# Thirty seven-product groups instead of twenty-five in a speech joint network, with a longer ring and evictions placed by the scheduler

## The chip, the cores and the metric

The kernel runs on one core of a Trainium2 chip. A core has five engines that run beside each other, each through its own queue in order: TensorE (PE, matrix products into PSUM), VectorE (DVE), ScalarE (ACT), GpSimd (POOL) and SyncE (SP, which here only issues transfers). The metric is the device time of one execution in microseconds, as a median of several runs.

## The reference, cut to what matters

Two audio sequences x of 4000 steps and 512 channels go through two convolutions of five taps, each followed by a gelu and by taking every second step; 1000 steps f per sequence are left. Eight label vectors g per sequence come beside them. Both are projected, every step is combined with every label by a tanh, and the result is projected again:

```
f  = gelu(conv5(gelu(conv5(x, w1))[::2], w2))[::2]      # (2, 1000, 512)
fe = f @ w_f;  ge = g @ w_g                              # (2, 1000, 512), (2, 8, 512)
j  = tanh(fe[:, :, None, :] + ge[:, None, :, :])         # (2, 1000, 8, 512)
out = j @ w_o                                            # (2, 1000, 8, 512)
```

All operands are bf16. The last line is 16000 rows of 512 by a matrix of 512 x 512.

## The kernel before, in words

**Stages.** The first convolution and most of the second fill about the first half of the time. They use transforms that need fewer products than five taps; one unit of the second convolution (class `Unit`, steps `s1` to `s5`) makes nine times four products of 334 columns for one batch and one quarter of the channels, evicted by ACT and DVE. `fe` (L908) projects f: eight times four products of 501 columns per batch, evicted by ACT for odd and by DVE for even quarters m.

**The joint stage.** The 16000 rows (label by label, 1000 steps each) are cut into 125 tiles of 128. `tanh(v, k)` (L919) makes, on ACT, the k-th quarter of the channels of label v: 1000 columns, 64 such calls. It writes into a ring jT of 3072 columns, so a call that crosses the ring's end is cut in two; a slot can be written again only when the products that read it are done.

**Plain tiles.** `Plain.go` (L1034) makes one tile with four products of 512 columns, one eviction to ost and the store.

**Groups of seven products.** `Seven` makes four tiles together, as a 2 x 2 block product in Strassen's manner (Winograd's form): seven products of half size instead of eight. Each is four matmuls of 256 columns (two row tiles, two k). Its operands are tiles of jT, sums of tiles (`sums`, L1062: three on POOL that follow from each other, one on DVE, all into one of four buffers ss, in fp16) and sums of quarters of w_o (tw, made once on POOL). Of the seven results, three are copied from PSUM to SBUF (`keep`, buffers sn), three are added to such a copy by DVE into the output buffer og (`out` with v), one is copied to og (`p4`). A bank is used further after its copy: product 6 adds to the bank of product 1 once that was copied, 7 to that of 6, 4 to that of 7 once DVE has added it, 3 to that of 5.

**Order.** The loop at L1186 gives the groups in this order: p1 of a group, p7 of the one before, p5, p2, a filler, the sums of the next group, p6, p4 of the one before, p3, a filler. Fillers are, for the first 13 groups, what is left of the second convolution and fe of the second batch (18 pieces), and then two plain tiles for each of ten groups. The last two groups have none. After the fe of the first batch (L1168) come the rest of conv unit 12 and 13, then two plain tiles, then the groups.

**The scheduler.** This order is not yet that of the engines. `Plan.schedule` (L150) is a list scheduler with a cost for each instruction: for PE, POOL and SP it takes, of the instructions that are ready, the first in the order written; for ACT and DVE the one with the earliest due time. Before, each instruction's engine is fixed when it is written: products 1, 6 and mostly 5 are copied by ACT, plain tiles by DVE, product 4 mostly by DVE.

The functions that the diff touches, with the profile's line numbers:

Of the kernel before, what the change touches and what calls it, by code (L numbers as in the profile page):

```python
# [63 lines left out]
class Op:  # L64
    __slots__ = ("eng", "fn", "reads", "writes", "dma", "signal", "count", "sem", "val", "idx", "cost", "pin", "after", "wire")


class Plan:
# [11 lines left out]
    def op(self, eng, fn, reads=(), writes=(), cost=0.1):  # L80
        o = Op()
        o.eng, o.fn, o.dma, o.signal, o.idx = eng, fn, False, False, len(self.ops)
        o.reads, o.writes, o.cost, o.pin, o.after = tuple(reads), tuple(writes), cost, self.pin, list(self.hold)
        self.ops.append(o)
        return o

    def dma(self, eng, fn, reads=(), writes=(), sem=None, nbytes=524288, rate=345e3):

        o = Op()
        o.eng, o.fn, o.dma, o.signal, o.idx = eng, fn, True, False, len(self.ops)  # L90
        o.reads, o.writes, o.cost, o.pin, o.after, o.wire = tuple(reads), tuple(writes), 0.43, True, [], nbytes / rate
        if sem is None:
            sem = [self.nc.alloc_semaphore(f"s_d{o.idx}"), 0]
        sem[1] += 16
        o.sem, o.val = sem[0], sem[1]
        self.ops.append(o)
        return o

    def edges(self):
# [26 lines left out]
        for o in ops:  # L126
            p = {}
            for j in np.flatnonzero(sbuf[o.idx, :o.idx] | psum[o.idx, :o.idx]).tolist():
                q = ops[j]
                if o.dma and q.dma and not set(x for v in o.writes for x in v.cells.tolist()) & set(  # L130
                        x for v in q.reads + q.writes for x in v.cells.tolist()):
                    continue
                same = q.eng == o.eng and not q.dma and not o.dma
                over = any(W[o.idx, c] > R[o.idx, c] and R[j, c] + W[j, c] > 0 or R[o.idx, c] > 0 and W[j, c] > 0
                           for c in range(na, na + 8))
                p[j] = not same or (bool(sbuf[o.idx, j] or over) and o.eng != "pe")
            for j in o.after:
                if ops[j].eng != o.eng or ops[j].dma:
                    p[j] = True
                else:  # L140
                    p.setdefault(j, False)
            if o.pin:
                j = last.get(o.eng)
                if j is not None:
                    p.setdefault(j, False)
                last[o.eng] = o.idx
            pred.append(p)
        return pred

    def schedule(self, pred):  # L150
# [20 lines left out]
        cand = {e: [] for e in free}  # L171
        for i in range(n):
            if not left[i]:
                cand[ops[i].eng].append(i)
        order = {e: [] for e in free}
        wire, start = 0.0, [0.0] * n
        for _ in range(n):
            best = None
            for e, c in cand.items():
                if c:  # L180
                    t = max(free[e], min(ready[i] for i in c))
                    if best is None or t < best[0]:
                        best = (t, e)
            t, e = best
            now = [i for i in cand[e] if ready[i] <= t + 0.02]
            i = min(now, key=(lambda i: i) if e in ("pe", "sp", "pool") else (lambda i: (late[i], i)))
            cand[e].remove(i)
            order[e].append(i)
            o = ops[i]
            start[i] = t  # L190
            free[e] = t + o.cost
            end = free[e]
            if o.dma:
                wire = max(wire, t + 1.8) + o.wire
                end = max(wire, t + 2.0)
            for s in succ[i]:
                ready[s] = max(ready[s], end + HOP if pred[s][i] else free[e])
                left[s] -= 1
                if not left[s]:
                    cand[ops[s].eng].append(s)  # L200
# [4 lines left out]
    def emit(self, block, tail):  # L205
        nc, ops = self.nc, self.ops
        pred = self.edges()
        order = self.schedule(pred)
        pos = {i: p for e in order for p, i in enumerate(order[e])}
# [69 lines left out]
def bass_standalone__seq2seq_rnn_t_joint__speech_kernel(  # L279
# [29 lines left out]
    RING = 3072  # L309
# [5 lines left out]
    with ExitStack() as es:  # L315
# [45 lines left out]
        jT = at("jT", [NK, RING], BF16, w1_off)  # L361
# [556 lines left out]

        def tanh(v, k):  # L919

            b, u = v // U, v % U
            lo, hi = v * T2, (v + 1) * T2
            while lo < hi:
                n = min(hi - lo, RING - lo % RING)
                t = lo - v * T2
                act(jT[k, lo % RING:lo % RING + n], feT[b][k, t:t + n], ACT.Tanh,
                    bias=geT[k * BU + v:k * BU + v + 1])
                lo += n
# [50 lines left out]
        nu = len(units) - 2  # L979
# [28 lines left out]
        def evict(eng, o, v):  # L1008
            if eng == "act":
# [15 lines left out]
        class Plain:  # L1025
# [8 lines left out]
            def go(self, last=False):  # L1034
                r0, s = self.jt * P % RING, self.s
                for h in range(2 if last else 1):
                    w = H if last else NT
                    cl = slice(h * w, (h + 1) * w)
                    bk = take()
                    v = ps.cols(bk * NT, w)  # L1040
                    mm(v, [(jT[k, r0:r0 + P], wo_sb[k, cl]) for k in range(NK)], True, True)
                    evict("act" if h else "dve", ost[s][cl], v)
                    free.append(bk)
                    store(self.jt, lambda a, b: ost[s].rows(a, b, cl), ("p", s), ("sp", "act")[h], cl)

        class Seven:
# [4 lines left out]
            def __init__(self, jt):  # L1051
                self.jt, self.n = jt, Seven.count
                Seven.count += 1
                assert jt % 2 == 0 and RING % (2 * P) == 0
                self.c = [(jt + 2 * r) * P % RING for r in range(2)]
# [3 lines left out]
            def a(self, r, k):  # L1059
                return jT[2 * k:2 * k + 2, self.c[r]:self.c[r] + H]  # L1060

            def sums(self):  # L1062
                S = self.S
                for eng, i, x, y, op in (("pool", 0, self.a(1, 0), self.a(1, 1), add),
# [3 lines left out]
                    tt(eng, S[i], x, y, op)  # L1068

            def product(self, i, bk, start, check=False):  # L1070

                tile = lambda r, t, k: jT[k, self.c[r] + t * P:self.c[r] + (t + 1) * P]
# [35 lines left out]
            def p1(self):  # L1108
                self.A = take()
                self.product(1, self.A, True)  # L1110
                self.s1 = self.keep("act", self.A)

            def p5(self):
                self.D = take()
                self.product(5, self.D, True)
                self.d5 = self.keep("dve" if self.n < NF and self.n % 2 == 0 else "act", self.D)
# [7 lines left out]
            def p6(self):  # L1124
                self.product(6, self.A, False)
                self.u2 = self.keep("act", self.A)
# [11 lines left out]
            def p4(self, last=False):  # L1138
                self.product(4, self.A, False)
                self.out(1, 0, self.A, None, "act" if self.n >= NF and self.n % 4 == 0 else "dve")  # L1140
# [3 lines left out]
        pend, state = [], [1, 0]  # L1144

        def tanhs(upto, spread=None):

            while state[0] < B * U and not pend and state[0] * T2 < upto + 900:
                pend.extend((state[0], k) for k in range(NK))
                state[0] += 1  # L1150
            while pend and (pend[0][0] * T2 < upto or spread):
                v = pend[0][0]
                fits = (v + 1) * T2 - RING <= state[1] or (v + 1) * T2 <= RING
                if v * T2 >= upto and not fits:
                    break
                assert fits
                tanh(*pend.pop(0))
                spread = None
                if not pend and state[0] < B * U and state[0] * T2 < upto:
                    pend.extend((state[0], k) for k in range(NK))  # L1160
                    state[0] += 1

        conv = [f for u in units[nu:] for f in (u.s1, u.s2, u.s3, u.s4, u.s5)]
        conv += [lambda h=h, m=m: fe(1, h, m) for h in range(2) for m in range(NK)]
        NF = 13
        assert len(conv) == 18
        wosums()
        for h in range(2):  # L1168
            for m in range(NK):
                fe(0, h, m)  # L1170
        units[nu - 1].s3()
        units[nu - 2].s5()
        for k in range(NK):
            tanh(0, k)
        units[nu - 1].s4()
        units[nu - 1].s5()
        seven = [Seven(2 + 4 * i) for i in range(NF)] + [Seven(2 + 4 * NF + 6 * i) for i in range(12)]
        rest = [conv[2 * i:2 * i + 2] for i in range(5)] + [[f] for f in conv[10:]]
        rest += [[Plain(q.jt + 4).go, Plain(q.jt + 5).go] for q in seven[NF:-2]]
        rest += [[], []]  # L1180
        assert seven[-1].jt + 5 == ntile
        Plain(0).go()
        Plain(1).go()
        tanhs(seven[0].jt * P + NT)
        seven[0].sums()
        for i, (q, r) in enumerate(zip(seven, rest)):  # L1186
            p = seven[i - 1] if i else None
            state[1] = (p or q).jt * P
            base = q.jt * P
            last = i + 1 == len(seven)  # L1190
            tanhs(ntile * P if last else seven[i + 1].jt * P + NT)
# [9 lines left out]
            tanhs(base, True)  # L1201
            q.p6()
            if p:
                p.p4()
            q.p3()
            for f in r[1:]:
                f()
        seven[-1].p7()
        Plain(ntile - 7).go()
        seven[-1].p4(True)  # L1210
        Plain(ntile - 6).go()
        Plain(ntile - 1).go(True)
# [30 lines left out]
```

## Time and profile before

| | |
|---|---|
| median of 3 runs | 258.11 us (257.48 to 258.82) |
| the profiled execution | 256.91 us |
| its span, first to last instruction | 254.4 us |
| PE busy in the span | 248.9 us (98%) |
| DVE busy | 216.1 us (85%) |
| ACT busy | 205.4 us (81%) |
| POOL busy | 93.8 us (37%) |
| fe of the first batch starts on PE | 124.1 us |
| first tile of the joint stage starts on PE | 135.5 us |
| granted TensorE clock | 0.999 |

The profile is of one execution; its instructions carry a line, which for most is that of a helper (L402 products, L394 ACT, L389 two-input operations on DVE and POOL, L1012 copies by DVE), so they are told apart by the tiles they write and read: `og<-acc,sn` is DVE's add, `sn<-acc` a copy, `ss<-jT` a sum, `jT<-feT,geT` a tanh, `acc<-tw,ss` a product of a group. A row's length is from an instruction's start to its end; where the next one on the same engine starts earlier, the two overlap. In a merged row with "x4" the length is that of the four together.

### The profile page before, as it was taken

The page shows a single profiled execution, that of the slowest core. Times are in us where ns is not written, and L with a number is a line of the kernel's source. Part 1 is how long each engine was busy: PE and PEld are TensorE (multiplying, and loading weights), DVE is VectorE, ACT ScalarE, POOL GpSimd, SP SyncE. Part 2 cuts the span into 40 slices and gives each one's busy share as a digit, 9 for nine tenths or more (in the row PEclk, how much of TensorE's full clock was granted, in tenths as well). Part 3 has the DMA queues.
Part 4 walks back from the last instruction along what each step waited for, and adds up shares of the span by engine and source line. Part 5 has one row for each costly group of instructions (what it writes and reads, how often), then busy time and mean ns, then how long its engine had stood idle before and what let it go on. Part 6 is the DMA issues. An engine that isn't in the chain of part 4 may idle for free.

```text
span 254.4 us, 5113 instructions
## 1 busy us (share of the span) xinstructions
PE 248.9 (98%) x1850; PEld 178.2 (70%) x1850; DVE 216.1 (85%) x342; ACT 205.4 (81%) x321; POOL 93.8 (37%) x97
## 2 busy tenths in 40 slices
PE   8899999999999999999999999999999999999994
PEld 4799954456666666667556788787787777777782
DVE  1999999999999999495345878899998998799884
ACT  2667787569989766984489999799999998999751
POOL 1000000000000000002406999989854973974930
PEclk9999999999999999999999999999999999999999
DMA  7999999976000043000000134225435455454555
GB/s 249 339 166 231 168 207 197 174 211 206 3 0 0 3 126 123 3 0 3 0 1 31 54 103 144 87 85 168 146 106 165 146 157 195 150 191 139 167 185 186
DMA packets 56709, 31.86 MB, mean 125 GB/s; under 512 B 33630, under 2 KB 56430, under 8 KB 56686
## 3 DMA queue, kind: packets, MB, share of 16 engines
q1 hardware_dynamic: 56398, 31.36, 45.6%
q8 instruction: 14, 0.23, 0.4%
q10 hardware_dynamic: 288, 0.20, 0.3%
q14 instruction: 9, 0.07, 0.1%
HBM read 7.87 MB, written 16.38 MB: 95 GB/s over the span
## 4 chain that ended last, share of the span: by engine, by line
PE 69%; DVE 8%; ACT 7%; SPq 6%; DMA 5%; issue 3%; ACTq 0%; DVEq 0%
PE acc L402 69%; SPq L434 6%; ACT row L394 3%; DMA xs<-in_x_dram 2%; DVE acc L551 2%; DMA w_sb<-in_w_dram 2%; ACT hT L394 1%; DVE xt L389 1%; DMA xr<-in_x_dram 1%; DVE xp L389 1%; ACT sd L394 1%; DVE ssum L551 1%; ACT w_sb L394 1%; DVE ty L389 1%; ACT w_x L394 1%
## 5 line engine op out<-in xcount | busy, mean ns | idle before, releaser
L394 ACT ACTIVATE jT<-feT,geT 128x1000 bf16<-128x1000 f32 (+10 forms) x84 | 76.9, 956 | 3.1 <-DVE feT L917 2.1
L389 DVE TENSOR_TENSOR og<-acc,sn 128x512 bf16<-128x512 f32 x75 | 50.3, 683 | 7.3 <-PE acc L402 4.2
L402 PE MATMUL acc<-wo_sb,jT 128*128 128x256 bf16 (+1 forms) x304 | 52.2, 306 | 0.0
L394 ACT ACTIVATE sn<-acc 128x512 f32<-128x512 f32 x68 | 40.9, 618 | 4.2 <-PE acc L402 4.2
L402 PE MATMUL acc<-tw,ss 128*128 128x256 f16 x300 | 41.1, 273 | 0.0
L389 POOL TENSOR_TENSOR ss<-jT 128x512 f16<-128x512 bf16 x25 | 29.5, 1191 | 30.9 <-ACT jT L394 30.9
L402 PEld LDWEIGHTS acc<-wo_sb,jT 128*128 128x128 bf16 x304 | 29.7, 98 | 11.8
L402 PEld LDWEIGHTS acc<-tw,ss 128*128 128x128 f16 x300 | 29.2, 98 | 7.6
L389 POOL TENSOR_TENSOR ss<-ss,jT 128x512 f16<-128x512 f16 x25 | 29.8, 1206 | 0.7
L389 POOL TENSOR_TENSOR ss<-jT,ss 128x512 f16<-128x512 bf16 x25 | 29.3, 1181 | 0.7
L402 PE MATMUL acc<-row,w_sb 128*128 128x334 bf16 x160 | 29.2, 305 | 0.0
L386 POOL MEMSET hT<- 128x8 bf16 (+2 forms) x6 | 0.7, 147 | 73.3 <-ACT hT L394 68.4
L402 PE MATMUL acc<-xt,w_sb 128*128 128x252 bf16 (+1 forms) x144 | 23.2, 305 | 0.0
L402 PEld LDWEIGHTS acc<-row,w_sb 128*128 128x128 bf16 x160 | 15.5, 97 | 6.9
L1012 DVE CAST ost<-acc 128x512 bf16<-128x512 f32 (+1 forms) x25 | 16.8, 674 | 4.0 <-PE acc L402 3.6
L389 DVE TENSOR_TENSOR ss<-jT 128x512 f16<-128x512 bf16 x25 | 19.1, 763 | 0.2
L402 PEld LDWEIGHTS acc<-xt,w_sb 128*128 128x128 bf16 x144 | 14.1, 98 | 5.9
L402 PE MATMUL acc<-hT,w_t 128*128 128x334 bf16 x96 | 17.6, 305 | 0.0
L402 PE MATMUL acc<-xp,w_sb 128*128 128x334 bf16 x96 | 17.5, 304 | 0.0
L1012 DVE CAST og<-acc 128x512 bf16<-128x512 f32 x22 | 15.1, 686 | 2.7 <-PE acc L402 2.5
L394 ACT ACTIVATE hT<-acc 128x334 bf16<-128x334 f32 (+2 forms) x21 | 11.6, 559 | 6.9 <-PE acc L402 6.9
L402 PE MATMUL acc<-fT,wf_sb 128*128 128x501 bf16 x64 | 15.1, 375 | 0.0
(91 smaller groups left out, 442.6 us busy)
## 6 DMA issues: line engine op xcount, KB each, us to landing
out_dram<-og SPq DMA_DIRECT2D x86, 128.0 KB, 2.0
w_sb<-in_w_dram SPq DMA_DIRECT2D x10, 512.0 KB, 5.2
out_dram<-ost SPq DMA_DIRECT2D x22, 128.0 KB, 2.0
xr<-in_x_dram SPq DMA_DIRECT2D x2, 512.0 KB, 3.8
wf_sb<-in_w_f_dram SPq DMA_DIRECT2D x1, 512.0 KB, 4.0
wg_sb<-in_w_g_dram SPq DMA_DIRECT2D x1, 512.0 KB, 5.0
wo_sb<-in_w_o_dram SPq DMA_DIRECT2D x1, 512.0 KB, 5.8
out_dram<-og SPq DMA_DIRECT2D x2, 120.0 KB
```

The costliest lines, as they stand in the source:

```text
L386: pl.op("pool", lambda e: e.memset(v.ap, 0.0), (), (v,))
L389: pl.op(eng, lambda e: e.tensor_tensor(out=o.ap, in0=a.ap, in1=b.ap, op=op), (a, b), (o,), 0.02 + 2.14e-3 * o.ap.free_size() if eng == "po ...
L394: pl.op("act", lambda e: e.activation(o.ap, i.ap, func, scale=scale, bias=0.0 if bias is None else bias.ap), rd, (o,), o.ap.free_size() * ...
L402: ins = e.matmul(o.ap, lhsT=l.ap, rhs=r.ap, start=start and n == 0, stop=stop and n == len(pairs) - 1, skip_group_check=not check)
L434: pl.dma("sp", lambda e: e.dma_start_transpose(out=dst.ap, in_=src), (), (dst,), nbytes=(hi - lo) * 2 * D, rate=185e3)
L551: pl.op(eng, lambda e: e.scalar_tensor_tensor(out=o.ap, in0=a.ap, scalar=f, in1=b.ap, op0=ALU.mult, op1=add), (a, b), (o,), vec_cost(o, (a ...
L1012: pl.op("dve", lambda e: e.tensor_copy(out=o.ap, in_=v.ap), (v,), (o,), vec_cost(o, (v,)))
```

## The change

- Thirty groups of seven products instead of 25, and five plain tiles instead of 25. Tiles 0 and 1 stand before the groups and the last three after them.
- The loop over conv units stops one unit earlier (13 instead of 14 of 16); the fe of the first batch follows the last step of unit 11 and the third of unit 12. What then is left of the convolution and the fe of the second batch (22 pieces) fills the first thirteen groups; the last seventeen have no filler. The two fe are called quarter by quarter, both halves of one together.
- The ring gets a second part: jX, 2560 columns in the place of the second convolution's weights, used from column 6144 on. Both are counted in blocks of 256 columns (`slot`, `owner`).
- tanh calls beyond the need of the next group are given two at a time as far as the ring has room (`tanhs`), those of the second batch only when its fe has been written.
- A copy can be written for ACT or DVE (`Plan.flex`): the scheduler gives it to the engine whose turn comes first. The three copies of a group, that of product 4 and those of plain tiles are written so. The adds stay on DVE.
- The planner's cost of DVE's sum is set to 0.70 us.
- The end: the last tile's first half goes before the last product 4, its second half after the last plain tile.

The core of the diff:

```diff
+    def flex(self, alt, reads, writes):
+
+        o = self.op(next(iter(alt)), None, reads, writes, max(c for _, c in alt.values()))
+        o.alt = alt
+        return o
...
-            cand[e].remove(i)
+            for f in engines(i):
+                cand[f].remove(i)
             order[e].append(i)
             o = ops[i]
+            if o.alt:
+                o.eng, (o.fn, o.cost), o.alt = e, o.alt[e], None
...
-    RING = 3072
+    JB = 2 * P
+    RING, WIDE, XB = 12, 10, 24
...
-        jT = at("jT", [NK, RING], BF16, w1_off)
+        jT = at("jT", [NK, RING * JB], BF16, w1_off)
+        jX = at("jX", [NK, WIDE * JB], BF16, w2_sb.end - w2_sb.bytes)
...
+        def slot(j):
+            if j < XB:
+                return jT, j % RING
+            j = (j - XB) % (WIDE + RING)
+            return (jX, j) if j < WIDE else (jT, j - WIDE)
...
-        nu = len(units) - 2
+        nu = 13
...
         def evict(eng, o, v):
-            if eng == "act":
+            if eng is None:
+                n = o.ap.free_size()
+                pl.flex({"act": (lambda e: e.activation(o.ap, v.ap, ACT.Copy), 0.05 + n * 0.833e-3),
+                         "dve": (lambda e: e.tensor_copy(out=o.ap, in_=v.ap), 0.065 + n * 1.04e-3)}, (v,), (o,))
...
                     tt(eng, S[i], x, y, op)
+                    if eng == "dve":
+                        pl.ops[-1].cost = 0.70
...
             def p1(self):
-                self.s1 = self.keep("act", self.A)
+                self.s1 = self.keep(None, self.A)
...
             def p5(self):
-                self.d5 = self.keep("dve" if self.n < NF and self.n % 2 == 0 else "act", self.D)
+                self.d5 = self.keep(None, self.D)
...
-                self.out(1, 0, self.A, None, "act" if self.n >= NF and self.n % 4 == 0 else "dve")
+                self.out(1, 0, self.A, None, None)
...
-        pend, state = [], [1, 0]
-
-        def tanhs(upto, spread=None):
+        pend = [(v, k) for v in range(B * U) for k in range(NK)]
+
+        def tanhs(upto, read, more=0):
...
+                room = all(owner(j) < 0 or (owner(j) + 1) * JB <= read for j in range(v * T2 // JB, -(-(v + 1) * T2 // JB)))
...
-        seven = [Seven(2 + 4 * i) for i in range(NF)] + [Seven(2 + 4 * NF + 6 * i) for i in range(12)]
-        rest = [conv[2 * i:2 * i + 2] for i in range(5)] + [[f] for f in conv[10:]]
-        rest += [[Plain(q.jt + 4).go, Plain(q.jt + 5).go] for q in seven[NF:-2]]
+        S1 = 15
+        jts = [2 + 4 * i for i in range(S1)]
+        j = 2 + 4 * S1
+        for n in range(15):
+            jts.append(j)
+            j += 4 + 2 * gaps.count(n)
+        seven = [Seven(j) for j in jts]
+        plains = [j for j in range(ntile) if not any(q <= j < q + 4 for q in jts)]
+        fill = ["cc"] * 9 + ["c"] * 6 + ["p"] * 15
...
-        seven[-1].p7()
-        Plain(ntile - 7).go()
-        seven[-1].p4(True)
-        Plain(ntile - 6).go()
-        Plain(ntile - 1).go(True)
+        Plain(plains[0]).go()
+        end = Plain(plains[2])
+        end.half(0, "dve", "sp")
+        seven[-1].p4(True)
+        Plain(plains[1]).go()
+        end.half(1, "act", "act")
```

## The prediction

> **What bounds the kernel now.** I read four views: the chain that ended last, busy time by stretch, the order of time around single instructions, and the groups. First the chain, in order of time (start, length, what):
>
> ```profile
> 73.23 72.00 PE acc L402 x510
> 145.24 0.06 issue
> 145.29 104.76 PE acc L402 x826
> ```
>
> From 73.2 to 250.0 us the end is set by TensorE (PE) alone, with one gap of 0.06 us. Work taken from PE in there shortens the kernel one for one, if everything else keeps up. Does it? The busy time in two stretches of the joint stage (length, then PE, PEld, DVE, ACT, POOL, clock, DMA share, GB/s):
>
> ```profile
> 195.00:216.00 21.00, 21.00 (x160) 15.37 (x158) 19.23 (x31) 20.18 (x30) 15.71 (x15) 1.00 0.53 171
> 216.00:243.00 27.00, 27.00 (x206) 20.00 (x205) 23.64 (x37) 25.15 (x40) 21.27 (x20) 1.00 0.51 166
> ```
>
> PE is never idle, but VectorE (DVE) is busy 42.9 of 48 us, ScalarE (ACT) 45.3 and GpSimd (POOL) 37.0: cover is thin. What one instruction costs its engine is the distance to the next start, not its row's length, since lengths overlap. PE, by the order of time:
>
> ```profile
> 163.81 1.01 PE L402 MATMUL acc<-fT,wf_sb 128*128 128x501 bf16 x4
> 164.66 0.60 PE L402 MATMUL acc<-tw,ss 128*128 128x256 f16 x4
> ...
> 196.81 0.60 PE L402 MATMUL acc<-wo_sb,ss 128*128 128x256 bf16 x4
> 197.25 1.46 PE L402 MATMUL acc<-wo_sb,jT 128*128 128x512 bf16 x8
> 198.55 1.04 PE L402 MATMUL acc<-tw,ss 128*128 128x256 f16 x8
> ```
>
> Four products of 501 columns take 0.85 us, four of 256 take 0.436 (196.81 to 197.25), so four of 512 take 1.30 - 0.436 = 0.866. DVE and POOL:
>
> ```profile
> 209.19 1.27 DVE L389 TENSOR_TENSOR og<-acc,sn 128x512 bf16<-128x512 f32 x2
> 210.39 0.41 DVE L389 TENSOR_TENSOR ss<-jT 128x512 f16<-128x512 bf16 x1
> 210.72 0.68 DVE L1012 CAST ost<-acc 128x512 bf16<-128x512 f32 x1
> ...
> 228.49 1.15 POOL L389 TENSOR_TENSOR ss<-jT,ss 128x512 f16<-128x512 bf16 x1
> 228.50 1.42 DVE L389 TENSOR_TENSOR ss<-jT 128x512 f16<-128x512 bf16 x1
> 229.84 0.68 DVE L389 TENSOR_TENSOR og<-acc,sn 128x512 bf16<-128x512 f32 x1
> ...
> L389 DVE TENSOR_TENSOR ss<-jT 128x512 f16<-128x512 bf16 x25 | 19.1, 763 | 0.2
> ```
>
> Two adds from PSUM take 1.20 us of DVE (209.19 to 210.39): 0.60 each; copies from PSUM show the same. DVE's sum into ss has no fixed price: 0.41 at 210.39, with POOL idle; 1.42 at 228.50, where it ended 0.28 us after the POOL instruction then running (228.49 + 1.15). Over all 25 sums in the order of time, 20 began while POOL ran and average 0.850; the other 5 average 0.416. The adds next to them stay at 0.67 to 0.69 whatever POOL does. For the queue, 0.075 us of a row is overlap: 0.775 with POOL running, 0.34 without, 0.69 for the mean of 0.763.
>
> **The change, part by part.** The profiled execution took 256.91 us (span 254.4), 1.2 us below the median of 258.11; I sum against the former and shift.
>
> PE work. A group of four tiles costs 28 products of 256 columns, 28 x 0.1091 = 3.06 us; the same four tiles done plainly cost 16 x 0.2165 = 3.46. Five more groups for twenty plain tiles: 5 x 0.41 = **-2.04 us**. No product of the convolutions or of fe is added or removed. All of it lies on the path.
>
> Earlier start. fe(0) moves ahead of five rows of four convolution products (0.567 us each by the rows after 73 us), so it starts 2.84 us sooner; five rows instead of eight stand between its end and the first tile, which so starts 4.54 us sooner, and the eight rows displaced go between the groups. PE runs through, so price 0. What covers the new place: fe(0) waits for the last fT gelu; after its product PE still has two rows, 1.13 us, against 0.18 + 0.45 + about 0.1 for the eviction. If ACT is held by one tanh (1.02 us) the price is 0.6 once; I keep 0 to +0.6. The first plain tile needs four tanh after the last fe; ACT's list of 1.02 per tanh and 0.475 per copy ends about 0.3 us before PE arrives.
>
> ACT. 84 tanh instructions before and after (the ring's new breaks only redistribute them), copies from PSUM 71 to 74: +1.4 us. The queue adds up to 114.8 us in the 124 from its first tanh: hidden. The longer ring lets it be 3900 columns ahead where the fill ends; with 3072 it could not, and this is why the last fifteen groups can do without filler at all.
>
> POOL. 75 sums become 90, at 1.19 (its three rows' mean): 107 us in the 115 from its first sum to the last group. From the tenth group on: 18 groups x 3 x 1.19 = 64.3 us in 66.9 of PE. It holds if POOL is then three groups ahead, which four ss buffers allow. It will hardly pause, though.
>
> DVE. The order of the changed kernel gives it 90 adds for 75, 50 copies for 53, 30 sums for 25. The stretch that decides runs from its copy of product 1 of the tenth group to its add of product 7 of the twenty-ninth, for which PE's product 4 waits. DVE's queue there holds 60 adds, 20 sn copies, 7 og copies, 2 feT copies and 18 sums: 89 x 0.601 + 18p = 53.5 + 18p. PE's own work between the two products is 576 x 0.1091 + 16 x 0.213 = 66.25. With 0.18 us from a product's end to DVE's start (a wait that recurs throughout the trace) and about 0.08 back, DVE is late by 0.26 + 53.5 + 18p - 66.25 = **18p - 12.5 us**. At p = 0.69 that is nothing; at 0.775 it is 1.45; at 0.34 DVE has time to spare. I take 0.775, since POOL will run nearly without pause: **+1.45**. Bounds: 0 (p at or below 0.69) and +5.7 (p = 1.01: the longer ten of the twenty rows average 1.087, less 0.075). The average of all twenty is nearest, because a sum's arrival has no tie to POOL's beat. The kernel before has no such stretch: with eight plain tiles to four groups its DVE queue, by the same reckoning, stays 0.4 us early everywhere, and no PE gap contradicts that.
>
> Here a rule speaks against the change. The Trainium skill, "SBUF — State Buffer", section "Who interferes with whom", says that a DVE instruction with two SBUF inputs and a GpSimd instruction that reads SBUF cannot share: whichever comes second is blocked until the first ends, while one SBUF input is left alone. The 0.28 us above and the untouched adds agree. Taken at its worst, every sum waiting for a whole POOL instruction, it would price p at 1.37 and the lateness at 12; the measured average, with sums that arrive anywhere in a POOL instruction, is what I use.
>
> Flexible evictions. The planner hands a copy to ACT or DVE; the adds stay on DVE and wait for copies on the other queue. Before, DVE waited three times for ACT's sn, 2.2 us in all. Price 0 where DVE would have idled anyway, +2.2 if as much falls into the full stretch; I take 0 for lack of a row that places it. The stores are the same 141 transfers on the same queues. At SP, 4.6 stores of 0.45 us per group of 3.06: hidden. The tail (last product to end, 3.4 us) keeps its form.
>
> Sum: -2.04 + 1.45 = **-0.6**: 256.3 for such an execution, 257.5 as a median.
>
> **The rivals.**
> 1. *The whole gain.* If sums meet POOL as they did on average (0.69), DVE is just in time: 256.1. For it: the group's mean of 0.763 is real. Against: it holds five sums that met an idle POOL, and with 15 more POOL sums there will be few such.
> 2. *Slower: POOL holds DVE's sums.* From p = 0.81 the gain is gone, from 0.88 the kernel is over 0.5% slower. At 0.95, midway from there to the upper bound: -2.04 + 4.6, 260.7. For it: rows of 1.27 to 1.42. Against: needs sums to begin early in a POOL instruction more often than before.
> 3. *Copies on two queues.* DVE, with no slack, waits for ACT's copies, 2.2 us on top of the forecast: 259.7.
> 4. *POOL becomes the bound.* With one group of lead instead of three it would be 2 x 3.57 - 2.6 = 4.5 us late: 260.6. Against: tanh is 3400 to 4100 columns ahead there, by the order of the queues.
>
> That the change does not do what it says can be left out: the count of PE's products is in its order.
>
> **How the numbers follow.** Forecast 0.50 (its own range 256.4 to 258.9), whole gain 0.20, rival 2 0.15, rival 3 0.10, rival 4 0.05. 0.5%, 1.29 us, is about what a measurement can tell here. Faster, below 256.8: rival 1 almost whole (0.19) and a sixth of the forecast (0.08), 0.27. Slower, above 259.4: 0.12 + 0.06 + 0.04 = 0.22. The rest, 0.51, is within. The range goes from just below rival 1 to 260.4, which leaves half of rivals 2 and 4 out.
>
> **What will show it.** Right: PE's own work 2.04 us less; DVE busy almost without gaps from about 178 to 245 us; sums near 0.85; PE gaps of 1 to 2 us in all, released by DVE, in the last seventeen groups and none before. Rival 1: no PE gaps. Rival 2: sums near 1 us. Rival 3: DVE waiting for sn in that stretch. Rival 4: PE waiting for ss from POOL. I am wrong altogether if PE waits around the new fe(0), or if the wait sits on tanh.

## The result, and the profile after

The changed kernel takes 258.35 us (median of 22 runs, 257.34 to 259.47); beside it on the same chips the kernel before took 257.65 (22 runs). The ratio is 1.0031, interval 1.0016 to 1.0047: slower by 0.3%, where the forecast was 0.6 us faster.

The head of the page of the changed kernel (its profiled execution took 257.83 us):

```profile
span 255.9 us, 5292 instructions
...
PE 249.3 (97%) x1910; PEld 182.6 (71%) x1910; DVE 227.2 (89%) x359; ACT 207.3 (81%) x324; POOL 111.6 (44%) x112
```

Busy time by stretch, the same two stretches as shown of before (start and end, length, then PE, PEld, DVE, ACT, POOL, clock, DMA share, GB/s):

```profile
195.00:216.00 21.00, 20.41 (x182) 16.93 (x180) 20.94 (x33) 20.50 (x32) 21.00 (x19) 1.00 0.50 161
216.00:243.00 27.00, 26.40 (x239) 22.53 (x238) 26.97 (x43) 22.94 (x39) 27.00 (x24) 1.00 0.49 159
```

DVE was busy 42.9 of these 48 us before and is now busy 47.9; POOL went from 37.0 to 48.0, without a pause. PE, never idle before, now loses 1.2 us here. The waits of PE from 195 us on (weight loads first, then products; total, times, longest, in us; a gap can appear in both lists):

```profile
PEld acc L421 <- DVE og L408: 2.2, 5, 0.7
PEld acc L421 <- DVE sn L1051: 0.9, 3, 0.4
PEld acc L421 <- ACT sn L1050: 0.6, 2, 0.5
PEld acc L421 <- POOL ss L408: 0.3, 1, 0.3
...
PE acc L421 <- DVE og L408: 0.8, 2, 0.5
PE acc L421 <- ACT sn L1050: 0.2, 1, 0.2
```

To size the gaps I take the distance between the starts of neighbouring products, less what a product of that width takes (0.1091 us for 256 columns, 0.2165 for 512, and so on). From 130 us on the kernel before has 0.22 us of gaps. The changed kernel has 3.07, and 2.93 of it lies after 200 us; the largest are 0.63 at 213.1 and 0.52 at 238.9. So -2.04 + 3.07 - 0.22 = +0.81 us, against 0.70 between the medians. That this sum comes within 0.1 us is partly luck. It leaves out what happens before 130 us and after the last product: in the two profiles fe of the first batch starts at 122.07 instead of 124.13 us, 2.06 sooner where 2.84 of work moved behind it. In the variants below the same sum misses the measured difference by up to 1.5 us, and once by 2.1.

Each gap over 0.03 us can be put down to what ended the wait of the product or of its weight load. Of the 3.07 us, DVE released 2.17 (1.66 its adds, 0.51 its copies), ACT's copies 0.41, POOL's sums 0.21; the rest are small. The four largest that DVE released (at 205.56, 213.13, 238.94 and 247.98 us) each come within 2.7 us of the start of a sum that took 1.27 to 1.40 us.

The gap at 213.13 us in the order of time, DVE, POOL and PE from 211 us on (start, length, engine; behind the bracket, the wait and its releaser):

```profile
211.04 2.46 POOL L408 TENSOR_TENSOR ss<-ss,jT 128x512 f16<-128x512 f16 x2
211.18 1.29 DVE L408 TENSOR_TENSOR ss<-jT 128x512 f16<-128x512 bf16 x1
212.40 0.67 DVE L408 TENSOR_TENSOR og<-acc,sn 128x512 bf16<-128x512 f32 x1
213.00 0.67 DVE L1051 COPY sn<-acc 128x512 f32<-128x512 f32 x1
213.12 0.33 PEld L421 LDWEIGHTS acc<-tw,jT 128*128 128x128 bf16 x4 [0.74 <-DVE og L408]
213.13 0.61 PE L421 MATMUL acc<-tw,jT 128*128 128x256 f16 x4 [0.46 <-DVE og L408]
```

DVE's sum begins 0.14 us after a POOL instruction and is done only at 212.47; the add behind it ends at 213.07, and product 4, which needs that add, starts at 213.13. Of the 30 sums 27 began while POOL ran, at a mean of 0.929 us (before: 20 of 25, 0.850); the other three took 0.412. The largest group of them, the one with operands in jT alone:

```profile
L408 DVE TENSOR_TENSOR ss<-jT 128x512 f16<-128x512 bf16 x18 | 16.8, 937 | 4.3 <-ACT jT L413 4.3
```

### The profile page after: what moved, and what is told of

The parts are those of the page before. It is cut to its first block, busy times and chain, and to the rows that moved or that the text cites. A ratio compares the mean times of both kernels' runs of the same rounds, so it can differ in the third digit from the quotient of the medians.

```text
span 255.9 us, 5292 instructions
## 1 busy us (share of the span) xinstructions
PE 249.3 (97%) x1910; PEld 182.6 (71%) x1910; DVE 227.2 (89%) x359; ACT 207.3 (81%) x324; POOL 111.6 (44%) x112
## 5 line engine op out<-in xcount | busy, mean ns | idle before, releaser
L408 DVE TENSOR_TENSOR og<-acc,sn 128x512 bf16<-128x512 f32 x90 | 58.8, 678 | 0.6 <-PE acc L421 0.2
L413 ACT ACTIVATE jT<-feT,geT 128x1000 bf16<-128x1000 f32 (+6 forms) x56 | 51.3, 969 | 0.5 <-DVE feT L936 0.4
L421 PE MATMUL acc<-tw,ss 128*128 128x256 f16 x360 | 49.5, 273 | 0.4 <-ACT sn L1050 0.2
L1050 ACT ACTIVATE sn<-acc 128x512 f32<-128x512 f32 x54 | 32.0, 614 | 4.9 <-PE acc L421 4.0
L421 PE MATMUL acc<-wo_sb,jT 128*128 128x256 bf16 (+1 forms) x184 | 29.3, 282 | 0.0
L1051 DVE COPY sn<-acc 128x512 f32<-128x512 f32 x36 | 24.5, 681 | 1.7 <-PE acc L421 1.6
L413 ACT ACTIVATE jX<-feT,geT 128x1000 bf16<-128x1000 f32 (+4 forms) x28 | 25.1, 915 | 0.0
L408 POOL TENSOR_TENSOR ss<-ss,jT 128x512 f16<-128x512 f16 x20 | 23.6, 1194 | 0.2
L421 PEld LDWEIGHTS acc<-wo_sb,jT 128*128 128x128 bf16 x184 | 18.0, 98 | 4.8
L421 PE MATMUL acc<-wo_sb,ss 128*128 128x256 bf16 x120 | 18.2, 273 | 0.0
```

The source lines that it names most:

```text
L408: pl.op(eng, lambda e: e.tensor_tensor(out=o.ap, in0=a.ap, in1=b.ap, op=op), (a, b), (o,), 0.02 + 2.14e-3 * o.ap.free_size() if eng == "po ...
L413: pl.op("act", lambda e: e.activation(o.ap, i.ap, func, scale=scale, bias=0.0 if bias is None else bias.ap), rd, (o,), o.ap.free_size() * ...
L421: ins = e.matmul(o.ap, lhsT=l.ap, rhs=r.ap, start=start and n == 0, stop=stop and n == len(pairs) - 1, skip_group_check=not check)
L1050: pl.flex({"act": (lambda e: e.activation(o.ap, v.ap, ACT.Copy), 0.05 + n * 0.833e-3), "dve": (lambda e: e.tensor_copy(out=o.ap, in_=v.ap) ...
L1051: "dve": (lambda e: e.tensor_copy(out=o.ap, in_=v.ap), 0.065 + n * 1.04e-3)}, (v,), (o,))
```

## The experiments

Two readings stood against each other at first. Theory A: PE waits because DVE is late, and DVE is late because its sums are held by POOL. Theory B: the loss comes from DVE's share of copies and the new hand-overs between ACT and DVE. A third, D, came later: POOL itself is too slow for the pace of the groups. "Gaps" are those of PE from 130 us on, as sized above.

### Taking the hold away

POOL's sums become instructions that write ss and read nothing, with the same planned cost and the same waits, so that the order on PE, ACT, DVE and SP is the changed kernel's. The sums' values, and with them the output, are left out of the computation.

```diff
+                    if eng == "pool":
+                        pl.op(eng, lambda e, o=S[i]: e.memset(o.ap, 0.0), (x, y), (S[i],),
+                              0.02 + 2.14e-3 * S[i].ap.free_size())
+                        continue
                     tt(eng, S[i], x, y, op)
```

> The changed kernel with POOL's three sums of each group replaced by POOL instructions that only write ss (zeros) and read nothing; they keep the sums' planned cost and waits, so the orders of PE, DVE, ACT and SP are the same. The sums on POOL are left out, so the output is not the reference's. Theory A (POOL's reading holds DVE's sum): the 30 sums on DVE fall from 0.93 to about 0.42 us each, DVE's queue is early by p = 0.34 (18 x 0.34 - 12.5, about -6 us), the 2.9 us of PE gaps after 200 us go to under 0.3, and the kernel takes about 2.8 us less than the changed one, 255.6 against 257.7 before (ratio 0.992). Theory B (DVE and ACT wait for each other's copies, whatever a sum takes): the sums fall too, but 2 us of gaps or more stay, ratio 1.000 or above. Theory C (POOL itself is late with ss): as A in time, but with the sums on DVE still long.

Measured: 255.21 us, ratio 0.9902 (0.9876 to 0.9927), gaps 0.44 us. The group of DVE's sums (count, total and mean length in ns):

```profile
L408 DVE TENSOR_TENSOR ss<-jT 128x512 f16<-128x512 bf16 x18 | 7.4, 417 | 4.3 <-ACT jT L413 4.3
```

The same two stretches of this run:

```profile
195.00:216.00 21.00, 21.00 (x193) 18.35 (x192) 19.55 (x35) 21.00 (x33) 11.67 (x24) 1.00 0.50 162
216.00:243.00 27.00, 27.00 (x249) 23.69 (x247) 25.09 (x46) 23.31 (x40) 9.82 (x20) 1.00 0.51 167
```

Against 0.937 us in the changed kernel's group of the same name, every sum takes 0.415 to 0.426 although POOL still runs, and PE is never idle in these stretches. Without POOL's reads the whole gain of the seven-product groups is there, and 0.7 us more than PE's work and gaps account for. B falls as the main cause. But POOL also became faster (0.47 us per instruction), so D is not yet excluded.

### Pricing the sum higher

The planner's price of a DVE sum is raised from 0.70 to 0.86.

```diff
-                        pl.ops[-1].cost = 0.70
+                        pl.ops[-1].cost = 0.86
```

> The changed kernel with the planner's price of DVE's sum at 0.86 instead of 0.70 us, the pitch that the profile after shows with POOL running (0.93 less 0.075). The planner then gives three sn copies and one plain copy more to ACT and orders both queues anew. Theory A: DVE has 2.4 us less in the full stretch, gaps of about 1 us stay, about 256.6 against 257.7 before (ratio 0.996). Theory B: more copies on ACT for DVE to wait for; no better than the change, 1.003 or above.

Measured: 258.36 us, 1.0023 (1.0007 to 1.0040), gaps 2.69. A's ratio is missed, and B's nearly met. The waits of PE from 195 us on:

```profile
PEld acc L421 <- ACT sn L1050: 1.4, 3, 0.7
PEld acc L421 <- POOL ss L408: 1.1, 4, 0.3
...
PEld acc L421 <- DVE sn L1051: 0.4, 1, 0.4
...
PE acc L421 <- POOL ss L408: 0.7, 2, 0.5
```

DVE was relieved of four copies and now releases 0.4 us of the gaps instead of 2.2, as A says. But ACT, which got them, releases 1.1 and POOL 0.6: the wait moved to other engines. That a constant price cannot tell the planner which sums will be long may be the reason; this run alone does not show it.

### Engines of the copies as before

```diff
-                self.s1 = self.keep(None, self.A)
+                self.s1 = self.keep("act", self.A)
...
-                self.d5 = self.keep(None, self.D)
+                self.d5 = self.keep("dve" if self.n < 13 and self.n % 2 == 0 else "act", self.D)
...
-                self.u2 = self.keep(None, self.A)
+                self.u2 = self.keep("act", self.A)
...
-                self.out(1, 0, self.A, None, None)
+                self.out(1, 0, self.A, None, "act" if self.n >= 13 and self.n % 4 == 0 else "dve")
```

> The changed kernel with the engines of the copies fixed as before (products 1 and 6 on ACT, 5 on ACT but for every second of the first 13 groups, 4 mostly on DVE, plain tiles on DVE). ACT gets 13 copies more (6.2 us) and DVE 13 fewer (7.8 us). Theory A: DVE has room for sums of 0.93, so no PE gap is released by DVE; but a group then needs 3 x 0.475 + 1.95 of tanh = 3.4 us of ACT against 3.06 of PE, so ACT takes DVE's place in the last fifteen groups, 2 to 4 us of gaps released by ACT, 258 to 260 (ratio 1.000 to 1.008). Theory B: with the choice gone the waits between the queues go too, gaps under 1 us, 256.5 (ratio 0.995).

Measured: 261.18 us, 1.0125 (1.0102 to 1.0149), gaps 3.61: slower than both theories gave. So the scheduler's choice of engines is worth 0.9% to the changed kernel, but most of it at the end: between the two profiled executions (260.44 and 257.83 us) 0.5 us are gaps and 2.0 lie behind the start of the last product, from which it is 5.72 us to the end instead of 3.72. The gaps are released mostly by DVE (2.6 us), where A had expected ACT. This run also shows something the prediction had excluded. DVE's sums between 199 and 214 us:

```profile
199.66 1.22 DVE L408 TENSOR_TENSOR ss<-jT 128x512 f16<-128x512 bf16 x1
203.20 1.21 DVE L408 TENSOR_TENSOR ss<-jT 128x512 f16<-128x512 bf16 x1
206.72 1.21 DVE L408 TENSOR_TENSOR ss<-jT 128x512 f16<-128x512 bf16 x1
210.25 1.21 DVE L408 TENSOR_TENSOR ss<-jT 128x512 f16<-128x512 bf16 x1
213.78 1.21 DVE L408 TENSOR_TENSOR ss<-jT 128x512 f16<-128x512 bf16 x1
```

They come every 3.53 us, each at the same place in a POOL instruction (0.93 us of it left), and each takes the same 1.21 to 1.22. 3.53 is not PE's pace (3.06 per group) but POOL's. POOL's start to start is 1.113 us, and 1.30 when a DVE sum ends inside the instruction; two of the one and one of the other make 3.53. DVE has no pause between these sums: 1.13 us from a sum to the next start and four instructions of 0.60 make the same 3.53, and PE waits for it three times, 1.0 us in all. The sum has fallen into step with the engine that holds it.

### Fewer groups

28 groups, with two plain tiles after the eighteenth, the twenty-first, the twenty-fourth and the twenty-seventh group (the numbers in `gaps` count from the sixteenth).

```diff
-        gaps = ()
+        gaps = (2, 5, 8, 11)
...
-        for n in range(15):
+        for n in range(13):
```

> The changed kernel with 28 groups instead of 30 and 13 plain tiles instead of five, eight of them two at a time after the groups 18, 21, 24 and 27 (counted from one). PE has 0.82 us more work than the changed kernel, 1.22 less than before. DVE loses six adds and two sums and gains three copies (about 3.5 us less). Theory A: DVE's queue is no longer full over the stretch, gaps under 0.5 us: 257.65 - 1.22 + 0.4, about 256.8 (ratio 0.997), the best of these. Theory B: gaps go down with the groups' share only, to about 2 us: 258.4 (ratio 1.003).

Measured: 259.42 us, 1.0059 (1.0040 to 1.0079), gaps 3.31: a miss, slower than with 30 groups. DVE had less to do, but its held sums were longer, 1.013 us in the mean. POOL and DVE's sum around 219 us:

```profile
218.19 1.15 POOL L408 TENSOR_TENSOR ss<-ss,jT 128x512 f16<-128x512 f16 x1
219.31 1.15 POOL L408 TENSOR_TENSOR ss<-ss,jX 128x512 f16<-128x512 f16 x1
219.53 1.20 DVE L408 TENSOR_TENSOR ss<-jT 128x512 f16<-128x512 bf16 x1
220.42 1.34 POOL L408 TENSOR_TENSOR ss<-jT,ss 128x512 f16<-128x512 bf16 x1
221.71 1.16 POOL L408 TENSOR_TENSOR ss<-jX,ss 128x512 f16<-128x512 bf16 x1
```

The sum waits until POOL's second instruction is done and ends 0.28 us later, at 220.73. The third POOL instruction has begun meanwhile and is held in turn: the next one starts 1.29 us after it, where the others are 1.11 to 1.12 apart. The next two sums, at 223.05 and 226.57, come in the same step of 3.52 us.

### Shorter POOL instructions

Each POOL sum is given as two instructions of 256 columns, in the changed kernel; as four of 128 (`H // 2` and `range(2)`); and as two in the kernel before.

```diff
+                    if eng == "pool":
+                        w = H // 1
+                        sub_ = lambda v, kk, q: View(v.ap[:, kk, q * w:(q + 1) * w], v.cells, v.psum)
+                        for kk in range(2):
+                            for q in range(1):
+                                tt(eng, S[i, kk, q * w:(q + 1) * w], sub_(x, kk, q), sub_(y, kk, q), op)
+                        continue
```

> The changed kernel, with each of POOL's three sums of a group of 512 columns given as two instructions of 256 columns. Theory A (a sum of DVE is held until the running POOL instruction ends, then takes 0.28 us): what is left of a running POOL instruction is at most about 0.6 us instead of 1.17, so DVE's sums take 0.55 to 0.62 us in the mean instead of 0.929; the queue pitch falls to about 0.52 and 18 x 0.52 - 12.5 is below zero: TensorE's gaps after 200 us under 0.6 us instead of 2.9, and the ratio to the kernel before 0.992 to 0.995. Theory B (DVE's lateness comes from its own share of copies, whatever its sums take): gaps as in the changed kernel, ratio 1.002 to 1.004. Theory D (POOL's own pace is the bound, the sums of DVE only follow): the two halves cost POOL more than one whole, so the gaps grow, ratio above 1.004.

> The changed kernel, with each of POOL's sums given as four instructions of 128 columns. Theory A: DVE's sums 0.45 to 0.52 us in the mean, TensorE's gaps after 200 us under 0.6 us, ratio 0.991 to 0.995, unless POOL's own time for four quarters is over 0.25 us above one whole: then POOL's three sums of a group take more than TensorE's 3.06 us for seven products by so much that the products wait for POOL, and the ratio is over 1.0 with TensorE's gaps released by POOL. Theory D: the second case, ratio over 1.006.

> The kernel before, with POOL's sums given as halves. The control of the run with halves in the changed kernel: TensorE has no gaps in the joint stage before, so shorter holds have nothing to give. Theory A: DVE's sums 0.50 to 0.60 us in the mean instead of 0.76, ratio 0.999 to 1.001. If halves are good for something other than the holds, this run is faster too, by 0.5% or more.

Measured: halves 263.86 us, 1.0243 (1.0215 to 1.0271), gaps 8.32; quarters 287.36, 1.1179 (1.1135 to 1.1222), gaps 30.7; halves in the kernel before 258.39, 1.0027 (1.0003 to 1.0051), gaps 0.43: no gain, as expected of it. With halves DVE's held sums did shrink, from 0.929 to 0.663 us, not quite to the 0.55 to 0.62 expected. But POOL's start to start is 1.113 us for 512 columns, 0.627 for 256 and 0.384 for 128, some 0.14 us for each instruction whatever its width. Three sums in halves are 3.76 us per group against PE's 3.06. The waits of PE in the run with halves, the longest group:

```profile
PE acc L421 <- POOL ss L408: 5.1, 10, 1.0
```

A piece of its chain that ended last (start, length, what):

```profile
209.78 4.39 POOL ss L408 x7
214.17 0.53 issue
214.70 2.62 POOL ss L408 x5
217.31 0.51 issue
217.83 4.07 POOL ss L408 x7
```

From 209.78 us on the end is set by POOL. Theory D holds for these runs, and rival 4 is what comes next once the holds are shorter.

### The short ring

```diff
-    RING, WIDE, XB = 12, 10, 24
+    RING, WIDE, XB = 12, 10, 120000
```

> The changed kernel, with the ring of tanh values at its old 3072 columns; thirty groups and the conv unit sooner are kept, the scheduler picks the copies' engines anew. Theory A: the ring has no part in the holds; with fewer columns ahead ScalarE can take fewer copies early, so DVE is later: gaps of 3 to 5 us after 200 us, ratio 1.003 to 1.010. If the longer ring is worth nothing, the ratio is the changed kernel's, 1.001 to 1.005.

Measured: 261.29 us, 1.0147 (1.0113 to 1.0182), gaps 6.14. The longer ring is worth 1.2% to the changed kernel, more than expected. Between the profiled executions 3.1 of the 4.0 us are gaps and 1.0 lies behind the start of the last product.

### A busier POOL in the kernel before

The last of POOL's three sums is made twice.

```diff
-                                         ("pool", 3, self.a(0, 1), S[1], sub)):
+                                         ("pool", 3, self.a(0, 1), S[1], sub),
+                                         ("pool", 3, self.a(0, 1), S[1], sub)):
```

> The kernel before, 25 groups, nothing of the change; POOL makes the last of its three sums of a group twice (the same values again), so that it is busy almost without pause, as in the changed kernel. Theory A (the holds alone make the loss): a held sum costs DVE what is left of POOL's instruction and 0.20 us of its queue, and the POOL instruction after it takes 1.29 instead of 1.11 us; DVE, just in time before, falls late from about 145 us on: TensorE's gaps in the joint stage 3 to 4 us instead of 0.2, ratio 1.011 to 1.016. Theory B (the loss needs the thirty groups' smaller room on DVE or the scheduler's new hand-overs): no gaps, ratio 0.999 to 1.002.

Measured: 261.71 us, 1.0141 (1.0111 to 1.0170), gaps 4.02, spread from 145 us on. The number is A's, but not the reason alone. PE's waits from 130 us on:

```profile
PEld acc L402 <- POOL ss L389: 3.0, 8, 0.6
PEld acc L402 <- issue: 1.1, 3, 0.5
PEld acc L402 <- DVE og L389: 1.1, 3, 0.5
```

Most of these waits, about half of the gaps, are released by POOL. The run shows that a saturated POOL costs as much as that without any of the change; it does not tell DVE's lateness from POOL's.

### A planner that knows the hold, and 29 groups

The scheduler gets the price that the traces show: a DVE sum costs 0.34 us with POOL idle, else what is left of POOL's instruction and 0.20, and the POOL instruction after it 0.18 more. `held` names DVE's sums.

```diff
             start[i] = t
+            if i in self.held:
+                o.cost = max(0.34, pool[1] + 0.2 - t) if pool[0] <= t < pool[1] else 0.34
+                dsum = t + o.cost
+            if e == "pool":
+                o.cost += max(0.0, min(0.18, dsum - t))
+                pool = (t, t + o.cost + 0.04)
             free[e] = t + o.cost
```

> The changed kernel with thirty groups; only the planner's price of a DVE sum is changed, from 0.70 us always to what the traces show: 0.34 while POOL is idle, else what is left of POOL's instruction and 0.20, and POOL's next instruction 0.18 longer. The order and the engines of the copies follow from it. Theory A: the list scheduler then hands copies to ACT where DVE will be held; TensorE's gaps after 200 us 1.3 to 1.9 us instead of 2.9, ratio 0.998 to 1.000. Theory B: as with the price of 0.86, 1.002 to 1.004.

Measured: 258.74 us, 1.0037 (1.0018 to 1.0057): a miss. The held sums fell to 0.858 us, and the gaps from 3.07 to 2.28, where 1.3 to 1.9 had been expected. The last product starts at 251.97 us against 252.23, yet the span is 257.1 against 255.9. What ends it is product 4 with a copy of 512 columns and its stores, where the changed kernel ends with a half plain tile. The chain in the last groups:

```profile
237.65 2.50 POOL ss L416 x3
240.15 1.01 issue
241.16 0.10 POOL ss L416
241.26 1.21 issue
242.47 1.16 POOL ss L416
243.62 0.14 issue
243.76 0.38 PE acc L429 x2
```

With DVE relieved, the chain goes through POOL: thirty groups leave POOL no pause, and at 3.34 to 3.53 us per group it has used up its lead by then. So the same price was tried with 29 groups, and 29 groups without the price. Two plain tiles stand after the twenty-third and two after the twenty-eighth group in the first, after the twentieth and the twenty-fifth in the second.

```diff
-        gaps = ()
+        gaps = (7, 12)
...
-        for n in range(15):
+        for n in range(14):
```

> The same price of a held sum, and 29 groups, with two plain tiles after the twenty-third and two after the twenty-eighth group. Theory A: two pauses of POOL and of the 3.06 us pace let DVE catch up: gaps in the joint stage under 0.5 us, TensorE's own work 1.63 less than before, ratio 0.993 to 0.995, better than both kernels. Theory B (28 groups gave 1.006 and thirty 1.003): 1.002 to 1.006.

> The changed kernel with 29 groups and the planner's price of 0.70 as it was; two plain tiles after the twentieth and two after the twenty-fifth group. Theory A: the planner, which doesn't know the holds, fills DVE as before: gaps 1.7 to 2.5 us, ratio 1.000 to 1.003. If a pause alone is the cure, without the price: gaps under 0.5 us, ratio 0.993 to 0.995.

Measured: with the price 255.95 us, 0.9921 (0.9896 to 0.9946), gaps 0.42; without 257.48, 0.9985 (0.9966 to 1.0003), gaps 2.52. Both ratios lie just beyond the better edge of what A expected (0.993 and 1.000). The held sums in the better one are not shorter (0.953 us in the mean, 0.956 without the price). As the pauses stood in other places, one more run has the price with the plain tiles after the twentieth and the twenty-fifth:

> 29 groups, the planner's price of a held sum, and the plain tiles after the twentieth and the twenty-fifth group, as in the run of 29 groups alone. If the price did it: gaps under 0.6 us and 0.991 to 0.995. If the place of the pauses did it: gaps of 1.7 to 2.5 us and 0.997 to 1.000, as without the price.

Measured: 255.08 us, 0.9870 (0.9842 to 0.9897), gaps 0.35. Its chain from 74 us to the last product:

```profile
74.82 176.20 PE acc L429 x1392
```

And the two stretches:

```profile
195.00:216.00 21.00, 21.00 (x190) 17.91 (x188) 21.00 (x36) 21.00 (x32) 19.13 (x17) 1.00 0.47 151
216.00:243.00 27.00, 27.00 (x237) 22.64 (x235) 26.93 (x41) 23.93 (x42) 27.00 (x24) 1.00 0.55 180
```

PE runs 176.20 us in one piece. With the pauses in the same place, the price alone took the gaps from 2.52 to 0.35 us. DVE was not given less: from 178 to 248 us it has 109 instructions here and 107 without the price, 17 of them sums in both, so what the price changed is their order and engine. DVE is as full as in the changed kernel, 47.9 of 48 us: fullness as such costs nothing, lateness does. This version beats both kernels. By PE's account it should gain 1.5 us (1.63 less work, 0.13 more gaps); 2.9 were measured, more than expected. Where the rest lies was not found: the part before 74 us differs by up to 1.6 us between profiles, and the profiled execution, 256.10 us, was the slowest of the seven.

### DVE's sum made longer without POOL

To tell DVE's lateness from POOL's pace, the first run of this section is taken (POOL only writes, nothing is held, POOL far ahead, orders the changed kernel's) and DVE's sum is lengthened by itself: six, eight or ten instructions over parts of the columns in place of one. The planner still sees one instruction at 0.70.

```diff
+                        def parts(e, o=S[i], x=x, y=y, op=op):
+                            for k in range(2):
+                                for q in range(4):
+                                    c = slice(H * q // 4, H * (q + 1) // 4)
+                                    ins = e.tensor_tensor(out=o.ap[:, k, c], in0=x.ap[:, k, c], in1=y.ap[:, k, c], op=op)
+                            return ins
+                        pl.ops[-1].fn = parts
                         pl.ops[-1].cost = 0.70
```

> The run with POOL's sums as writes only (output not the reference's), every engine's order the changed kernel's, with DVE's sum given as six instructions of 85 or 86 columns in place of one of 512. With 0.05 to 0.10 us for each further instruction the sum takes p = 0.59 to 0.84 of DVE's queue. Theory A (DVE's lateness is 18p - 12.5 us, whatever makes p): gaps after 200 us within 0.8 us of that formula at the measured p, none below p = 0.69. Theory D (POOL's pace made the gaps): no gaps at any p here, ratio 0.990 to 0.992.

> The same with eight instructions of 64 columns: p = 0.69 to 1.04. Theory A: the formula within 0.8 us: at p = 0.855 gaps of 2.9 us and a ratio of 1.002 to 1.004 as in the changed kernel, though no sum is held. Theory D: no gaps, ratio 0.990 to 0.992.

> The same with ten instructions of 51 or 52 columns: p = 0.79 to 1.24. Theory A: the formula within 1 us, at p = 1.0 gaps of 5.5 us and a ratio of 1.011 to 1.014. Theory D: no gaps, 0.990 to 0.992.

Measured, with p as the first start to the last end of a sum's instructions, less 0.075, over the 18 sums from 178 to 248 us:

| run | p, us | 18p - 12.5 | gaps from 190 us on | us | ratio (interval) |
|---|---|---|---|---|---|
| one instruction | 0.34 | -6.4 | 0.35 | 255.21 | 0.9902 (0.9876 to 0.9927) |
| six | 0.686 | -0.15 | 0.34 | 255.61 | 0.9916 (0.9888 to 0.9944) |
| eight | 0.844 | 2.7 | 2.05 | 257.33 | 0.9982 (0.9955 to 1.0009) |
| ten | 0.970 | 5.0 | 4.60 | 259.97 | 1.0071 (1.0046 to 1.0096) |
| changed kernel | 0.823 | 2.3 | 2.97 | 258.35 | 1.0031 (1.0016 to 1.0047) |

PE's waits in the run with ten:

```profile
PEld acc L421 <- DVE sn L1051: 3.0, 9, 0.6
PEld acc L421 <- DVE og L408: 3.0, 9, 0.8
```

The formula holds within 0.7 us over its whole range, with no more gaps at 0.686 than at 0.34, and with POOL busy less than half of the time. Theory D alone falls. The ratios with eight and with ten came out below what A expected (1.002 to 1.004, 1.011 to 1.014): all four runs with POOL only writing take 0.6 to 0.7 us less than PE's work and gaps account for, which was not explained. The changed kernel lies 0.7 us above the formula; the 2.17 us of gaps that DVE released are what the formula gives, and the rest was released mostly by ACT's copies and POOL's sums.

## Why the prediction was wrong, and where it was right

- *PE's work, -2.04 us.* Right: the run without holds shows the gain whole. With the gaps it accounts for the difference to 0.1 us, partly by luck, as said above.
- *Earlier start, 0.* Right: no gap over 0.1 us between 75 and 200 us, so none around the new fe(0). The conv unit's place was not tried by itself.
- *POOL, "It holds if POOL is then three groups ahead".* Right for the changed kernel, where PE waits 0.3 us for it, but nearly used up: 3.34 us per group without held instructions, 3.53 with one. Rival 4 is the next wait in line, as the halves and the thirty groups with the hold priced showed.
- *DVE, 18p - 12.5.* The mechanism, the place (from 200 us on, in the groups without filler, none before), the releaser and the formula were right; the runs in six, eight and ten pieces confirm break-even and slope. The failed step is the size of p, with the sentence "The average of all twenty is nearest, because a sum's arrival has no tie to POOL's beat". Taken was 0.775; the stretch has 0.823, past the break-even of 0.81 that the prediction itself named: two of its 18 sums met an idle POOL, but the 16 others took 0.960 us in the mean, where the kernel before had 0.850. The term is 2.3 us instead of 1.45, and DVE released 2.17 us of gaps. The tie was shown where it is plainest, in the runs with fixed engines and with 28 groups; in the changed kernel itself I see longer sums, but no such regular step, so how much of its 0.05 us is the tie and how much chance is open.
- *Flexible evictions, price 0 "for lack of a row that places it".* Right for the wait that it priced, DVE waiting for ACT's copies: from 178 to 250 us DVE waits for nothing but PE, 0.2 us in all. What came was a wait without a term in the sum: PE waiting for ACT's copies, 0.4 us of gaps. The run with the sum priced at 0.86 shows it larger, 1.1 us.
- *Sum.* With what was released by DVE (2.2 us), ACT (0.4), POOL (0.2) and small gaps (0.3), less the 0.2 of before, it is -2.04 + 2.9 = +0.8, measured +0.7. The forecast missed its sign mainly by the 0.7 to 0.85 us that its term for DVE was too small, inside its bounds, and by waits for ACT and POOL at which it had put nothing; the balance was nearer to even than a single forecast could say.

## What to carry to other kernels

Where one engine's work is held by another's, price it from the stage the change makes, not from the average of a stage in which the holder still paused: once the holder is saturated, the held work can fall into its step and meet the long end each time. A planner that prices the hold as a function of when the work starts can place what stands behind it, and a pause for the saturated engine then pays for itself (29 groups with that price beat 25 and 30; without it 29 were level with 25). A constant price, even the measured mean, moved the wait to other engines. Before shortening the holder's instructions, count what each instruction costs it whatever its width.

## What the runs showed of the hardware

- The hold works in both directions. A DVE sum of two SBUF operands ends 0.28 us after the POOL instruction that ran when it began (0.279 to 0.285 in 19 of the 20 of the kernel before; the other began 0.085 us before that end and took 0.41 in all). The POOL instruction during which a sum ends takes 1.30 us from start to start instead of 1.113 (20 and 53 instructions of the changed kernel). The Trainium skill, "SBUF — State Buffer", section "Who interferes with whom", says that a DVE instruction with two SBUF inputs contends with a GpSimd instruction that reads SBUF, that the shared port pair is an exclusive lock, and that the order of issue decides who blocks; the trace agrees on both sides. It says too that a GpSimd instruction that only writes does not contend: in the run with writes only, the sums took 0.415 to 0.426 us.
- A sum can miss its turn: in the changed kernel and six of its variants one sum, at about 171 us, began 0.004 to 0.024 us before the end of a POOL instruction and took 1.40 to 1.42 us, as long as one that meets a whole further instruction. One that began 0.055 us before it, in the run with fixed engines, took 0.415.
- POOL's two-input sums cost about 0.14 us each beyond their columns (0.384, 0.627, 1.113 us for 128, 256 and 512), so the quarters took 38% more of POOL than the wholes.
